# Score units of VectorE carried in ScalarE's score sets, two rings of three PSUM banks, one bank for the rest, and another order of the first loads

## The chip, the cores and the metric

The kernel runs on one core of one Trainium2 chip. The metric is the device time of that core in microseconds. Before the change three runs gave 744.49, 744.65 and 745.26 us, a median of 744.65.

## What is computed

Two attentions over the same x (2048 tokens, 512 columns, 32 heads of 16 columns), mixed by a gate. All tensors are bfloat16.

```python
def _A_ref(x, wqkv, wo):              # full attention, no mask
    qkv = (x @ wqkv).reshape(B, S, 3, H, Dh).transpose(2, 0, 3, 1, 4)
    q, k, v = qkv[0], qkv[1], qkv[2]
    p = softmax(einsum("bhqd,bhkd->bhqk", q, k) * Dh ** -0.5)
    o = einsum("bhqk,bhkd->bhqd", p, v)
    return o.transpose(0, 2, 1, 3).reshape(B, S, D) @ wo

def _B_ref(x, wqkv, wo):              # each token sees 8 tokens, 2 apart
    idx = pos[:, None] - (arange(8) * 2)[None, :]
    kg, vg = k[:, :, idx], v[:, :, idx]
    logits = einsum("bhsd,bhswd->bhsw", q, kg) * scale   # -1e9 where idx < 0
    o = einsum("bhsw,bhswd->bhsd", softmax(logits), vg)
    return o.transpose(0, 2, 1, 3).reshape(B, S, D) @ wo

g = sigmoid((x * gate_w).sum(-1, keepdims=True))
out = g * _A_ref(x, A_wqkv, A_wo) + (1 - g) * _B_ref(x, B_wqkv, B_wo)
```

## The kernel before, in words

**A planner writes the program.** The Python code holds a list of operations (`Op`) with an engine, a duration, what each depends on, a due time and the buffers (`Hold`, `Slots`) that it takes and gives back. `Sched.run` goes forward in planned time, takes for each engine the operation that can start soonest (among near ones the one due first) and emits it. `chain_on` ties each engine's instructions in that order, so the chip runs a fixed order on every engine; the chip's own semaphores decide when. `Policy` holds knobs of the planner; for each stretch of 8 us of planned time it is made from a seed in `CHOICES`. `Sched.warm` adds products with zeros where the plan has TensorE too idle.

**Full attention.** Heads come in 8 groups of four (`NG`), queries in 4 blocks of 512 (`QW`). A period is one pair of (query block, group); there are 32, in the order of `periods`. In a period the keys come in 16 tiles of 128 (`NT`). A score unit is one head, one key tile, one query block: a 32-row matmul whose 128x512 result fills one PSUM bank; TensorE runs the units of different heads in different strips of rows at once. A period has 64 units, the kernel 2048.

- ScalarE's units: `pe_source` proposes a fill of a ring (`fillA`, `emit_fill`), ScalarE reads it with one exponential over all its banks and writes `pT` (`act_source`), and TensorE multiplies `pT` with V into the period's accumulator `acc` (`emit_pva`). The rings `rA` (three banks) and `rB` (two) alternate (`ring_i`), so a set has three and two units in turn.
- VectorE's units: `start_quad` and `make_quad` take the four heads of a key tile from the back of a period, at most the last `TD` = 4 tiles. Each unit is a `fillD` on TensorE into one of two PSUM banks `m`, and a `conv` on VectorE, which makes a first term of the exponential by a multiply and an add on integers; two more terms (`term`) are adds over the whole quad (`dt`). TensorE multiplies the three terms with V and two weighted copies of V (`vd_row`, made for the last `TD` tiles by `weigh`). So a quad is four conversions and two terms on VectorE and twelve products on TensorE.

**PSUM** has eight banks: `rA` three, `rB` two, `acc` one, `m0` and `m1` one each. Everything else that TensorE makes goes through an `m` bank, and VectorE empties it: projections of K, Q and V, those of the local attention (`b_tile`), its sums (`bf2`, `vsum`) and the output projection (`final`).

**Local attention** (`b_tile`, 16 tiles of 128 tokens): K and V rows are stored to `kv_scr` in device memory and loaded again eight times shifted (`ksh`, `vsh`). GpSimd multiplies and sums; from tile `RELIEF` = 6 on, half of the sums over a head are taken by VectorE (`lred`). GpSimd and VectorE are ordered by hand (`lock`) where VectorE runs a fast operation.

**Start.** ScalarE's queue loads the weights of the first heads, ScalarE copies them into place (`wd`). `x_load` brings x transposed with eight DMA transposes on SP's queue, two halves of four. K of the first group is projected for all tokens (`k_proj` with `first`), two blocks in `m`, two in `rB`; the largest magnitude of each row (`kred`, `k_rows`) must be known for all tokens before the keys are completed (`fix`) and the first scores can be made. Q of the first block goes through `acc`.

**End.** The last query block's output projection is split: two tiles take a ring each once the last scores are read (`lent_final`, `lent_close`), two go through `m`.

Of the kernel before, what the change touches and what calls it, by code (L numbers as in the profile page):

```python
# [11 lines left out]
ALU = mybir.AluOpType  # L12
# [19 lines left out]
TD = 4  # L32
# [48 lines left out]
RELIEF = 6  # L81
# [47 lines left out]
class Policy:  # L129
    __slots__ = ("full", "press", "quads", "backlog", "heed", "near", "shift", "conv", "ring", "rng", "wobble", "warm", "tight", "late", "whole", "split")  # L130

    def __init__(self, seed):
        self.full, self.press, self.quads, self.backlog, self.heed = 5, -2000.0, 3, 3000.0, True
        self.near, self.shift, self.conv, self.ring, self.wobble, self.warm = 60.0, 0.0, -5000.0, 480.0, 0.0, 0.0
        self.tight, self.late, self.whole, self.split = 600.0, 2000.0, False, False
        self.rng = random.Random(seed)
        if seed:
# [16 lines left out]
            self.warm = pick(0.0, 0.04, 0.08, -0.03)  # L154

# [290 lines left out]
def kernel(  # L446
# [143 lines left out]
    S_.t["DVE"] = 2500.0  # L590
    S_.t["ACT"] = 2500.0
# [4 lines left out]
    def x_load(half):  # L596
# [36 lines left out]
    for kind, lo in (("k", D), ("q", 0)):  # L633
        w0[kind] = const.tile([128, DC, G1], BF16, name=f"w{kind}0")
# [11 lines left out]
    load("x0", x_load(0), 8100.0)  # L646
    load("x1", x_load(1), 13600.0)
    ld["x1a"] = S_.add(Op("SP", lambda: None, dur=1.0, due=-8.0, lat=13000.0, name="ld_x1a"))
    load("bw", dma(bw[:], B_wqkv.rearrange("(c p) n -> p c n", p=128)), 20500.0)
# [4 lines left out]
    load("gw", gw_load, 22000.0)  # L654
    load("wv", dma(wv[:, :, G1:D], a_w3[:, :, 2 * D + G1:3 * D]), 24000.0)
# [22 lines left out]
    S_.t["PE"] = 7800.0  # L678
    xt_ops = {sc: [ld[f"x{sc // 2}"]] for sc in range(NC)}
# [6 lines left out]
    def k_proj(m, sc, due, first=False):  # L686
        lent = first and sc >= 2
        if lent and not early:
            early["hold"] = Hold("rB")
        hold = early["hold"] if lent else Hold("m")  # L690
        st = {}

        def part(c0, c1):
            def s():
                if c0 == 0 and lent:
                    if sc == 2:
                        early["ps"] = ps.tile([128, 2, QW], FP32, tag="rB", bufs=1, name="ring")
                    st["pk"] = early["ps"][:, sc - 2, :]
                elif c0 == 0:
                    st["pk"] = misc_ps(hold, [128, QW])[:]  # L700
# [17 lines left out]
        slow = 2 if first and sc == 0 else 1  # L718
        p1 = Op("PE", part(0, 2), mms=COL4 * (2 * slow), deps=([ld["x1a"]] if lent else xt_ops[sc]) + [ld[("k", m)]], due=due, acq=[] if lent and sc > 2 else [hold], not_before=0.0 if first else due - 5000.0,
                begun=[early["op"]] if lent and sc > 2 else [], name="k1")  # L720
        p2 = Op("PE", part(2, DC), mms=COL4 * (2 * slow), deps=[p1] + (xt_ops[sc] if lent else []), due=due, name="k2")
        for o in (p1, p2):
            S_.add(o)
        if first:
            r = S_.add(Op("DVE", red, dur=700.0, deps=[p2], due=due, name="kred"))
            e = S_.add(Op("ACT", evac, dur=650.0, deps=[p2, r] + k_evs.get(m, [])[-1:], due=due, rel=[] if lent and sc == 2 else [hold], name="kev"))
            if lent and sc == 2:
                early["op"] = p1
            if lent and sc > 2:
                early["next"] = p2  # L730
# [78 lines left out]
    def q_proj(c_, f, due):  # L809
# [21 lines left out]
        def spread():  # L831
            v = st["qt"][:].bitcast(I32)
            V.stream_shuffle(out=v[:, 0, :], in_=v[:, 1, :], mask=LOWER)
            V.stream_shuffle(out=v[:, 1, :], in_=v[:, 1, :], mask=UPPER)

        def fold():
            for b in range(2):
                v = st["qt"][:, b, :].bitcast(U16)
                V.tensor_scalar(out=v, in0=v, scalar1=rowmask[:, b:b + 1], scalar2=None, op0=ALU.bitwise_and)
        ops = [Op("PE", part(0, 2), mms=COL4 * 2, deps=xt_ops[c_] + [ld[("q", f)]], due=due, acq=[hold, hq], name="q1"),  # L840
               Op("PE", part(2, DC), mms=COL4 * 2, due=due, name="q2"),
               Op("DVE", evac, dur=683.0, allow=300.0, rel=[hold], name="qev"),
               Op("DVE", spread, dur=860.0, allow=2000.0, name="qsh"),
               Op("DVE", fold, dur=486.0, lock=True, allow=2000.0, name="qabs")]
        S_.chain(ops)
        qb_ops[(c_, f)] = ops[1]
        for b in range(2):
            qt_ops[(c_, 2 * f + b)] = (ops[-1], hq)
# [47 lines left out]
    def b_tile(t, due):  # L896
# [190 lines left out]
        f = [Op("PE", vsum(c), mms=[("f", None, 132)] * W, allow=4000.0 if c == 0 else -3000.0, acq=[hb, obt_hold[t]] if c == 0 else [],  # L1087
# [127 lines left out]
    def lent_final(tt, due):  # L1215
# [6 lines left out]
        def step(lo, hi):  # L1222
            def s():
                if not lo:
                    lent["ps", tt] = ps.tile([128, 3 - tt, QW], FP32, tag=tag, bufs=1, name="ring")[:, 0, :]
# [126 lines left out]
    def pe_source(e):  # L1352
# [5 lines left out]
        n = 3 if ring_i[0] == 0 else 2  # L1358
        w = S_.slots[res].when()
        us = act_units(n)  # L1360
        if us and w < INF:
# [3 lines left out]
            if r < INF and S_.slots["pTA" if n == 3 else "pTB"].when() < INF:  # L1365
# [3 lines left out]
                op = Op("PE", None, mms=[("r", u[2], 512) for u in us], name="fillA")  # L1369
                op.fn = lambda us=us, res=res, n=n, op=op: emit_fill(us, res, n, op)  # L1370
# [372 lines left out]
```

## Time and profile before

| | |
|---|---|
| median of three runs | 744.65 us |
| the profiled execution: its time, its span | 744.69 us, 742.9 us |
| TensorE's granted clock | 1.00 |
| first exponential of scores starts | 19.46 us |
| exponentials of three banks, of two | 313, 312 (and one of one bank) |
| score units on ScalarE, on VectorE | 1564, 484 |
| instructions on VectorE, ScalarE, GpSimd | 1177, 658, 456 |
| GpSimd: time waited for VectorE's `dt`, ahead of `prod` | 139.9 us, in 64 waits |
| moved by DMA, mean rate | 47.42 MB, 64 GB/s |

The span is the time from the first instruction to the last of the profiled execution; its own time is 1.8 us longer. "Busy" of an engine is the time in which it runs at least one instruction; a duration reaches to an instruction's end, and on ScalarE, VectorE and TensorE the next begins before that, so durations add up to more than busy time. In a row of a group stand the line, the engine, the operation, what it writes and reads with shapes, the count, the busy time, the mean duration in ns, and the idle time of the engine just before, with what ended most of it. Every operation goes through one helper, so all rows have line 509; the tiles tell them apart. A page's group can mix shapes.

### The profile page before, as it was taken

The numbers are of one execution on the slowest core, as the hardware profiler recorded it, in microseconds if no ns is written. First come the engines' busy times: TensorE is split into PE (matmuls) and PEld (weight loads), VectorE is DVE, ScalarE is ACT, GpSimd is POOL, SyncE is SP. The second block draws the span as 40 slices with busy tenths as digits, with TensorE's granted clock in tenths as the row PEclk, the third lists the DMA queues.
The fourth block names the chain that finished last, engine by engine and source line by source line (L and its number), as shares of the span: only waits on it lengthen the run. The fifth ranks groups of instructions, "written<-read, shape, count | busy, mean of one in ns | idle before, by whom it ended". The sixth has DMA issues, their size and how long they took to land.

```text
span 742.9 us, 19546 instructions
## 1 busy us (share of the span) xinstructions
PE 695.6 (94%) x8110; PEld 247.9 (33%) x8110; DVE 652.9 (88%) x1177; ACT 719.2 (97%) x658; POOL 436.0 (59%) x456
## 2 busy tenths in 40 slices
PE   8899999999999989999999999999999999999897
PEld 2332332323323323333323333333333333323233
DVE  3888999798898898989999999989998988897963
ACT  2999999999999999999999999999999999999994
POOL 1066455756556666666655656657656557666660
PEclk9999999999999999999999999999999999999999
DMA  9413020120331201212132311121131113222100
GB/s 217 132 20 119 2 72 2 61 70 15 96 49 59 72 2 60 69 58 73 57 77 25 115 35 39 58 73 58 57 101 58 63 53 102 73 72 71 59 30 29
DMA packets 76232, 47.42 MB, mean 64 GB/s; under 512 B 37232, under 2 KB 73584, under 8 KB 76144
## 3 DMA queue, kind: packets, MB, share of 16 engines
q1 hardware_dynamic: 74288, 45.52, 20.9%
q8 instruction: 63, 1.03, 0.6%
q10 hardware_dynamic: 1856, 0.66, 0.3%
q14 instruction: 25, 0.20, 0.1%
HBM read 37.75 MB, written 6.32 MB: 59 GB/s over the span
## 4 chain that ended last, share of the span: by engine, by line
ACT 64%; PE 17%; issue 15%; DVE 5%; DVEq 0%; ACTq 0%
ACT pT L509 63%; PE m_ps L509 6%; PE acc L509 5%; PE ring L509 5%; DVE dt L509 2%; PE warm L509 1%; ACT lg L509 1%; DVE kt_all L509 0%; DVE accT L509 0%; DVE qt L509 0%; DVE kmax_all L509 0%; DVE lg L509 0%; DVE qb L509 0%; ACT kt_all L509 0%; DVE kvs L509 0%
## 5 line engine op out<-in xcount | busy, mean ns | idle before, releaser
L509 ACT ACTIVATE pT<-ring 128x1536 bf16<-128x1536 f32 x626 | 711.7, 1391 | 0.6 <-PE ring L509 0.4
L509 DVE TENSOR_SCALAR dt<-m_ps 128x512 uint16<-128x512 f32 x484 | 319.8, 680 | 32.8 <-PE m_ps L509 18.8
L509 PE MATMUL ring<-qt,kt_all 32*128 32x512 bf16 x1564 | 255.5, 381 | 36.1 <-ACT pT L509 28.8
L509 POOL TENSOR_TENSOR prod<-ksh,qb 128x512 f32<-128x512 bf16 x128 | 146.0, 1157 | 118.1 <-DVE dt L509 104.3
L509 PEld LDWEIGHTS <-kt_all 32*128 32x128 bf16 (+1 forms) x2304 | 99.9, 91 | 282.4 <-issue 265.1
L509 POOL TENSOR_TENSOR vsh<-vsh,lg 128x512 bf16<-128x512 bf16 x128 | 137.9, 1099 | 64.4 <-DVE dt L509 54.3
L509 DVE TENSOR_SCALAR dt<-dt 128x2048 uint16<-128x2048 uint16 x242 | 166.2, 702 | 3.6 <-PE acc L509 2.0
L509 PE MATMUL m_ps<-qt,kt_all 32*128 32x512 bf16 x484 | 165.3, 382 | 3.3 <-DVE dt L509 1.6
L509 PE MATMUL acc<-pT,vp_row 128*32 128x512 bf16 x1564 | 153.3, 387 | 0.7 <-DVE accT L509 0.3
L509 POOL TENSOR_TENSOR prod<-prod 128x512 f32<-128x512 f32 x88 | 96.2, 1101 | 41.1 <-DVE dt L509 35.6
L509 PEld LDWEIGHTS <-vp_row 128*32 128x32 bf16 x2048 | 49.9, 94 | 100.2 <-issue 91.2
L509 PE MATMUL acc<-dt,vd_row 128*32 128x512 bf16 x968 | 79.8, 381 | 0.0
L509 PE MATMUL m_ps<-bw,xT 128*32 128x512 bf16 x768 | 55.1, 382 | 0.1
L509 PE MATMUL acc<-dt,vp_row 128*32 128x512 bf16 x484 | 48.0, 386 | 1.1 <-DVE accT L509 1.1
L509 PEld LDWEIGHTS <-xT 128*32 128x32 bf16 (+1 forms) x1152 | 32.9, 96 | 27.3 <-issue 19.4
L509 POOL TENSOR_TENSOR ott<-accT,rden 128x256 bf16<-128x256 f32 x31 | 19.7, 635 | 33.8 <-DVE dt L509 28.0
L509 PE MATMUL m_ps<-ident,vsh 128*128 128x128 bf16 x512 | 37.4, 220 | 0.0
L509 PEld LDWEIGHTS <-vsh 128*128 128x128 bf16 x512 | 28.7, 98 | 11.8 <-issue 10.6
L509 PEld LDWEIGHTS <-vd_row 128*32 128x32 bf16 x968 | 25.0, 96 | 21.9 <-issue 9.3
L509 PE MATMUL acc<-ones_t,zw 128*32 128x512 bf16 x332 | 30.7, 387 | 0.0
L509 DVE TENSOR_REDUCE lg<-prod 128x32 f32<-128x512 f32 x40 | 26.5, 672 | 0.0
L509 DVE CAST kvs<-m_ps 128x512 bf16<-128x512 f32 x32 | 21.5, 675 | 4.6 <-PE m_ps L509 4.5
(79 smaller groups left out, 363.1 us busy)
## 6 DMA issues: line engine op xcount, KB each, us to landing
ksh<-kv_scr SPq DMA_DIRECT2D x16, 1024.0 KB, 5.7
vsh<-kv_scr SPq DMA_DIRECT2D x16, 1024.0 KB, 5.4
kv_scr<-kvs SPq DMA_DIRECT2D x16, 256.0 KB, 2.1
out_dram<-osb SPq DMA_DIRECT2D x14, 128.0 KB, 1.7
bw<-in_B_wqkv_dram SPq DMA_DIRECT2D x1, 1536.0 KB, 8.1
bwo<-in_B_wo_dram SPq DMA_DIRECT2D x1, 512.0 KB, 7.2
woarr<-in_A_wo_dram SPq DMA_DIRECT2D x8, 64.0 KB, 2.3
wv<-in_A_wqkv_dram SPq DMA_DIRECT2D x1, 384.0 KB, 8.6
```

The source lines that it names most:

```text
L509: return chain_on(key, f(*a, **k))
```

## The change

It has six parts.

1. `rB` has three banks like `rA`, and one `m` bank is left. The buffers `pT` become six of one size, shared by both rings.
2. A fill of a ring may carry one unit of VectorE (`rider`, `take_ride`): two units for ScalarE in the first two banks, one for VectorE in the third. `rider` takes it where a quad is open, its operands are there, and VectorE is planned to end the conversion within `ride` = 900 ns of the fill. `apart` declares the two readers independent. The ring is given back when both have read (`ring_read`). A unit that doesn't ride goes through `m` as before.
3. `TD` is 5, `RELIEF` is 3, the seeds in `CHOICES` are others. Quads may start from 17.5 us of planned time, before from 22.
4. The first 1024 tokens of x are loaded as they lie (`xn_load`) and transposed by TensorE with the identity (`x_turn`), through `rA`, `acc`, `rB` and `m`; ScalarE and VectorE empty them. The other 1024 come by four DMA transposes. The first projections of K use `rA`, `rB`, `m` and `acc`. GpSimd copies the first weights in place of ScalarE; three start buffers share memory with later ones. Seven warm-up matmuls accumulate in one group, before ten single ones.
5. The first Q block is emptied by ScalarE, and its two halves are spread and masked one after the other, so that the first can be used sooner.
6. The local sums (`bf2`) of the last two tiles are due 4 us earlier.

The diff, cut to its core:

```diff
-TD = 4
+TD = 5
...
-RELIEF = 6
+RELIEF = 3
...
+        self.ride = 900.0
...
-    for name_, n_ in (("m", 2), ("rA", 1), ("rB", 1), ("acc", 1), ("pTA", 3), ("pTB", 3), ("qt", 2), 
+    NPT = 6
+    for name_, n_ in (("m", 1), ("rA", 1), ("rB", 1), ("acc", 1), ("pT", NPT), ("qt", 2), 
...
+    PLAIN = 2
+    xn = work.tile([128, PLAIN * TPC, D], BF16, name="xn", tag="ksv_0", bufs=1)
+
+    def xn_load(q):
 
         def s():
-            lo, hi = half * S // 2, (half + 1) * S // 2
-            for c in range(DC):
-                SP.dma_start(out=xT[:, c, lo:hi], in_=x2d[lo:hi, c * 128:(c + 1) * 128], transpose=True)
+            SP.dma_start(out=xn[:, TPC * q:TPC * (q + 1), :], in_=x2d[q * QW:(q + 1) * QW, :].rearrange("(p t) c -> p t c", t=TPC))
+        return s
+
+    def x_load(c0, c1):
+
+        def s():
+            for c in range(c0, c1):
+                SP.dma_start(out=xT[:, c, PLAIN * QW:S], in_=x2d[PLAIN * QW:S, c * 128:(c + 1) * 128], transpose=True)
         return s
...
-            A.copy(out=o[:, c], in_=_ap(src[:, c, :], [list(src.ap[0]), [DH, 4], [4 * DH, 2], [1, DH]]))
+            G.tensor_copy(out=o[:, c], in_=_ap(src[:, c, :], [list(src.ap[0]), [DH, 4], [4 * DH, 2], [1, DH]]))
...
-    for k in range(10):
-        jt = ps.tile([128, QW], FP32, tag="acc", bufs=1, name="warm")
-        mm(jt[:], ones_t[:, 0:128], ones_t[:], True, True)
+    jt = ps.tile([128, QW], FP32, tag="acc", bufs=1, name="warm")
+    for k in range(7):
+        mm(jt[:], ones_t[:, 0:128], ones_t[:], k == 0, k == 6)
...
+    def x_turn(q, parts):
+        ends = []
+        for n_, (tag, cs, eng) in enumerate(parts):
+            hold, st = Hold(tag), {}
+
+            def turn(tag=tag, cs=cs, hold=hold, st=st):
...
+                for k, c in enumerate(cs):
+                    o = st["ps"][:, k, :].rearrange("d (p t) -> d t p", t=TPC)
+                    for tt in range(TPC):
+                        mm(o[:, tt, :], xn[:, TPC * q + tt, c * 128:(c + 1) * 128], ident[:], True, True)
+
+            def evac(cs=cs, eng=eng, st=st):
+                o, i = xT[:, cs[0]:cs[-1] + 1, q * QW:(q + 1) * QW], st["ps"][:, 0:len(cs), :]
+                if eng == "ACT":
+                    A.copy(out=o, in_=i)
+                else:
+                    V.tensor_copy(out=o, in_=i)
...
+    x_turn(0, (("rA", (0, 1, 2), "ACT"), ("acc", (3,), "DVE")))
+    x_turn(1, (("rB", (0, 1, 2), "DVE"), ("m", (3,), "ACT")))
...
-            V.tensor_copy(out=st["qt"][:, 1, :], in_=st["q"][:])
+            (A.copy if first else V.tensor_copy)(out=st["qt"][:, 1, :], in_=st["q"][:])
...
-        f = [Op("PE", vsum(c), mms=[("f", None, 132)] * W, allow=4000.0 if c == 0 else -3000.0, acq=[hb, obt_hold[t]] if c == 0 else [],
+        f = [Op("PE", vsum(c), mms=[("f", None, 132)] * W, allow=(4000.0 if t < NT - 2 else 0.0) if c == 0 else -3000.0, acq=[hb, obt_hold[t]] if c == 0 else [],
...
-        n = 3 if ring_i[0] == 0 else 2
+        n = 3
...
+                with_ = rider(us, max(r, S_.t["PE"])) if n == 3 and len(us) == 3 else None
+                if with_ is not None:
+                    us = us[:2]
...
+    def rider(us, at):
+
+        if not S_.policy.ride or S_.now < 17500.0:
+            return None
+        for q in quads_open:
+            k = next((k for k in range(4) if q["fops"][k].start is None), None)
+            if k is None:
+                continue
+            f_ = q["fops"][k]
+            if k == 0 and S_.slots["dt"].when() > at:
+                return None
+            if any(d.vis is None or d.vis > at for d in f_.deps) or any(d is not None and d.start is None for d in f_.begun):
+                return None
+            S_.guesses = {}
+            vis = at + 440.0
+            free = max(vis, S_.t["DVE"], S_.guess(q["aops"][k - 1]) if k else 0.0)
+            if free + 683.0 > vis + S_.policy.ride:
+                return None
+            used = {u[2] for u in us[:2]}
+            j = min(q["heads"], key=lambda j: (j in used, S_.pe_busy[j], j))
+            return f_, j, q, k
+        return None
+
+    def apart(peer, inst):
+
+        if peer is None:
+            return
+        if peer:
+            tc.declare_no_dep(inst.ins, peer[0].ins, reason="two engines read different banks of one set")
+        peer.append(inst)
+
+    def take_ride(op, ring, with_):
+        f_, j, q, k = with_
+        q["heads"].remove(j)
+        st = q["sts"][k]
+        st["j"], st["s"], st["peer"] = j, ring[:, 2, :], []
+        S_.pend["PE"].remove(f_)
...
+        conv = q["aops"][k]
+        conv.rel = []
+        return conv, st["peer"]
...
+    def ring_read(f_, t):
+        f_["reads"] -= 1
+        f_["free"] = max(f_["free"], t)
+        if not f_["reads"]:
+            S_.slots[f_["res"]].give(0, f_["free"])
...
-            if dve + max(0.0, S_.t["DVE"] - S_.now) < S_.policy.backlog and S_.now > 22000.0:
+            if dve + max(0.0, S_.t["DVE"] - S_.now) < S_.policy.backlog and S_.now > 17500.0:
```

More of the change, by code (lines that the diff above doesn't have):

```diff
@@ L129 @@
 class Policy:
-    __slots__ = ("full", "press", "quads", "backlog", "heed", "near", "shift", "conv", "ring", "rng", "wobble", "warm", "tight", "late", "whole", "split")
+    __slots__ = ("full", "press", "quads", "backlog", "heed", "near", "shift", "conv", "ring", "rng", "wobble", "warm", "tight", "late", "whole", "split", "ride")
     def __init__(self, seed):
@@ L686, in k_proj @@
     def k_proj(m, sc, due, first=False):
[L687 to L690, printed above, removed]
+        lent = first and sc < PLAIN
+        tag = ("rA", "rB")[sc] if lent else "acc" if first and sc == NC - 1 else "m"
+        hold = Hold(tag)
         st = {}
@@ L694, in s @@
             def s():
[L695 to L700, printed above, removed]
+                if c0 == 0:
+                    st["pk"] = ps.tile([128, 3, QW], FP32, tag=tag, bufs=1, name="ring")[:, 0, :] if lent else ps.tile([128, QW], FP32, tag="acc", bufs=1, name="p1")[:] if tag == "acc" else misc_ps(hold, [128, QW])[:]
                 pk = st["pk"]
@@ L836, in fold, with spread, s @@
-        def fold():
-            for b in range(2):
[L838 to L844, printed above, removed]
+        def spread(bs):
+            def s():
+                v = st["qt"][:].bitcast(I32)
+                for b in bs:
+                    V.stream_shuffle(out=v[:, b, :], in_=v[:, 1, :], mask=(LOWER, UPPER)[b])
+            return s
@@ L847, in q_proj @@
         for b in range(2):
-            qt_ops[(c_, 2 * f + b)] = (ops[-1], hq)
+            qt_ops[(c_, 2 * f + b)] = (ops[4 if first and not b else -1], hq)
     g_done = []
@@ L1364, in pe_source @@
                 r = max(r, qt_ops[periods[p]][0].vis, kdep(p, t).vis if kdep(p, t).vis is not None else INF)
-            if r < INF and S_.slots["pTA" if n == 3 else "pTB"].when() < INF:
+            if r < INF and sum(w_ < INF for w_ in S_.slots["pT"].free) > len(filled):
                 act_idle = S_.t["ACT"]
@@ L1700, in after_post @@
                 final(c_, tt, NPR - 1, NPR, now)
[L1703 to L1705 removed]
+    reds0 = [k_proj(0, sc, 40.0 + sc, first=True) for sc in range(NC)]
+    k_rows(0, reds0, 50.0, 1, 35000.0)
+    q_proj(0, 0, 40.5)
     for tb in (0, 8):
```

131 lines of the change are left out of this document (85 added, 46 removed), and 16 rows, old and new, of the table CHOICES.

## The prediction, made before the changed kernel was run

> **What bounds the kernel now.** I read the page first, then its groups kept apart by shape for ScalarE, the waits, the busy time in stretches, and the order of time at the start and the end.
>
> From the page:
>
> ```profile
> PE 695.6 (94%) x8110; PEld 247.9 (33%) x8110; DVE 652.9 (88%) x1177; ACT 719.2 (97%) x658; POOL 436.0 (59%) x456
> L509 ACT ACTIVATE pT<-ring 128x1536 bf16<-128x1536 f32 x626 | 711.7, 1391 | 0.6 <-PE ring L509 0.4
> L509 DVE TENSOR_SCALAR dt<-m_ps 128x512 uint16<-128x512 f32 x484 | 319.8, 680 | 32.8 <-PE m_ps L509 18.8
> L509 DVE TENSOR_SCALAR dt<-dt 128x2048 uint16<-128x2048 uint16 x242 | 166.2, 702 | 3.6 <-PE acc L509 2.0
> L509 PE MATMUL acc<-ones_t,zw 128*32 128x512 bf16 x332 | 30.7, 387 | 0.0
> ```
>
> ScalarE is the bound: its exponentials fill 711.7 of 742.9 us and it idles 0.6 us ahead of them. VectorE does 484 of the 2048 score units (121 quads of four), ScalarE the other 1564. The last row is padding that TensorE issues with nothing better to do: its 94% has 30.7 us of room.
>
> ScalarE by shape:
>
> ```profile
> L509 ACT ACTIVATE pT<-ring 128x1536 bf16<-128x1536 f32 x313 | 502.8, 1606 | 0.5 <-PE ring L509 0.4
> L509 ACT ACTIVATE pT<-ring 128x1024 bf16<-128x1024 f32 x312 | 367.3, 1177 | 0.1
> ```
>
> A third unit adds 1606 - 1177 = 429 ns. The durations overlap (502.8 + 367.3 is over 711.7), so the price of a set is what is left: 711.7 - 1564 x 0.429 = 40.7 us, over 626 instructions 65 ns, waiting included. A unit costs 0.429 us and the number of sets hardly matters.
>
> Busy time in stretches (PE, PEld, DVE, ACT, POOL), and the waits:
>
> ```profile
> 160.00:280.00 120.00, 113.37 (x1291) 39.07 (x1290) 109.45 (x200) 120.00 (x109) 73.63 (x77) 1.00 0.17 45
> 731.00:743.00 12.00, 8.03 (x141) 4.57 (x137) 4.75 (x8) 2.58 (x4) 0.00 (x0) 1.00 0.13 45
> ```
>
> ```profile
> PE ring L509 <- ACT pT L509: 28.8, 90, 0.8
> DVE dt L509 <- PE m_ps L509: 18.8, 36, 1.4
> PE m_ps L509 <- DVE dt L509: 1.6, 6, 0.4
> ```
>
> In the middle ScalarE never rests and VectorE is busy 109.45 of 120. TensorE waits for ScalarE to give a ring bank back, and almost never for VectorE: two m banks keep the two engines apart.
>
> Start and end in order of time:
>
> ```profile
> 0.72 11.14 SPq L509 DMA_TRANSPOSE xT<-in_A_x_dram  x8
> 10.77 2.46 PE L509 MATMUL m_ps<-xT,wkd 128*32 128x512 bf16 x24
> 14.60 1.91 PE L509 MATMUL ring<-xT,wkd 128*32 128x512 bf16 x32
> 18.55 1.38 DVE L509 TENSOR_SCALAR kt_all<-kt_all,rows,kadd 128x512 bf16<-128x512 bf16 x4
> 19.46 5.97 ACT L509 ACTIVATE pT<-ring 128x1536 bf16<-128x1536 f32 x5 [0.44 <-PE ring L509]
> 731.34 1.96 PE L509 MATMUL m_ps<-ident,vsh 128*128 128x128 bf16 x32
> ```
>
> So the time is three pieces in a row: 19.5 us until the first exponential, 712 of exponentials, 11 of ending. A change must move one of them.
>
> **The change part by part.**
>
> *Units moved to VectorE.* TD = 5 and the rides let VectorE take more. A quad costs it 4 x 319.8/484 + 2 x 166.2/242 = 4.02 us and saves ScalarE 4 x 0.429 = 1.72. RELIEF 3 gives VectorE 12 more reductions at 672 ns, 8.1 us, and takes tree sums from GpSimd, idle for over 300 us; the fifth weighted tile adds under 1 us. VectorE was busy 640 us from 20 to 731 us, 90% (652.9 less 7.8 and 4.8 in the ends). Of a middle of some 705 us: at 90% still, it has 635 - 640 - 9 = -14 us, 3.5 quads fewer; at 100% it has +56, 14 more. I take the middle, five more: 126 quads, 95%. What speaks for over 90% is the 32.8 us that VectorE idles ahead of score units, which now come with every set. TensorE does two more passes of four matmuls for each further quad (some 0.2 us each), 2 us for five, covered by the 30.7 us of padding; without that cover 2 us.
>
> *Sets.* The rings become three banks each and m one. With 1544 units on ScalarE and R rides there are (1544 + R)/3 sets. m can carry at most this: some 120 other evictions hold it for a 1.05 us projection and 0.69 us of reading, 210 us; what is left of 705 at 0.38 + 0.68 us a unit is 467. So R lies between 40 and 504 and the sets between 528 and 683, against 626: -6.4 to +3.7 us at 65 ns. I take R = 260, 601 sets. Exponentials: 1544 x 0.429 + 601 x 0.065 = 701.4, against 711.7: **-10.3**.
>
> *The new wait.* A ring bank set is free only when both engines have read it. Behind a fill that waits, TensorE's whole queue stands (products with V, projections), and ScalarE waits for the fill. The slack: while the other set is read (two units and the price of a set, 0.92 us) the next fill needs 0.38 and its signal, some 0.45; about 0.45 remains. A conversion late by one VectorE instruction (0.68) holds ScalarE for 0.23 us. Bounds: nothing, and every ride late, 260 x 0.23 = 60. The nearest row, units through two banks, has TensorE waiting for VectorE in 6 of 484 cases; the room is smaller now and VectorE fuller, so I take one ride in eight: 32 x 0.23, **+7.5**.
>
> The Trainium skill, "PSUM — Partial Sum Buffer", section "PSUM bank collisions raise a hardware error", says that two engines collide only on one bank and quadrant and that different banks run clean. By it the two readers cost each other nothing; no row shows two engines reading neighbouring banks of one set, and the sum is the same. Its general note to evacuate promptly speaks against the single m bank.
>
> *Start.* Half of x is loaded plainly and turned on TensorE (32 small matmuls, four evictions split over ScalarE and VectorE); four DMA transposes remain of eight. Those are issued 1.39 us apart and land 3.6 to 4.6 after issue, so the last landed near 14.2. Now two plain issues of 0.6 and three transposes stand ahead of the last: 0.7 + 1.2 + 4.2 = 6.1, landing 9.7 to 10.7. From there only 16 matmuls remain (0.95 us at the rate of the 14.60 row), two reductions at 0.69, the maximum (0.7), the first fix and the fill (0.83): about 4, first exponential near 14.2. That is -5.3. The weight copies moved from ScalarE to GpSimd (eight; nearest row there 0.43 each) end before 8 us, under the loads; the plain load's landing, 4 to 6 us, is hidden by the transposes as well.
> It hangs on TensorE's rate: the 24 matmuls at 10.77 took 2.46 us, the 32 at 14.60 only 1.91. At the slow rate the five first projections, 80 matmuls, take 8.2 us from about 8: first exponential near 18.7, -0.8. The rate rose near 12.9 us, 3.4 us after matmuls began to run unbroken at 9.5, although the ten warm-up ones, each waiting for the last, ran from 1.4. The change lets seven run unbroken and the turns follow, so I take the fast end with a little taken off: **-5.0**.
>
> The Trainium skill, "TensorE: Matmul & The Clock Gate", Part 1, has the clock rise some 3.4 to 4 us after sustained work begins. Counted from 1.4 us, the trace disagrees (still slow at 12); counted from 9.5 it agrees, and by it the change is fast from about 6 us.
>
> *End.* The last tiles' 32 matmuls (1.96 us at 731.34) stood after the last score fill, ahead of the products that close the accumulator. A due time 4 us earlier may put them under the exponentials: 0 to -2.0, I take **-1.0**; what is late next is the accumulator's transpose and the projections, as now.
>
> **Sum**: -10.3 + 7.5 - 5.0 - 1.0 = -8.8. The profiled execution took 744.7 us for its span of 742.9 (1.8 around it), the median is 744.65: forecast **735.9 us**.
>
> **The rivals.**
>
> *Late conversions hold the rings* (slower). The wait above, in ScalarE's stream: VectorE at 95% in a fixed order, with instructions ahead of a ride that wait for GpSimd or DMA. It cancels the gain at 7.5 + 8.8 = 16.3 us, 71 of 260 rides late, and decides from there. With half late: 130 x 0.23 = 30, 758 us; typically 750 to 760. For it: m's two banks hid such lateness, as the 1.6 us show. Against: a ride is taken only where VectorE is expected to end within 0.9 us of the fill, and ScalarE's own two units take 0.92.
>
> *VectorE takes no more units.* It stays near 90% with the reductions added, or the single bank starves it. 118 quads: 1576 x 0.429 + 612 x 0.065 = 715.9, +4.2; with +7.5 - 6.0 it is 750; with 121 quads 1564 x 0.429 + 608 x 0.065 = 710.5, -1.2, and 745.0. For it: 9 us in 120 idle are spread over many waits. Against: the supply of units no longer hangs on m.
>
> *VectorE nearly fills.* 132 quads: 1520 x 0.429 + 593 x 0.065 = 690.6, -21.1; with 7.5 and -6.0: 725.
>
> *Few rides happen, not what the change says.* m then carries all it can, 467 units (117 quads), with 528 sets: 1581 x 0.429 + 528 x 0.065 = 712.6, +0.9, no new wait, -6: 739.6. The order would be two-bank work through one bank, with VectorE idling ahead of dt.
>
> **How the numbers follow.** Forecast 0.48 (its own range 730 to 741); late rings 0.17 (over 746); no more units 0.16 (741 to 751); full VectorE 0.13 (721 to 730); few rides 0.06 (735 to 744). About 0.2% (1.5 us) is what a measurement can tell from no change. Faster: 0.48 + 0.13 + 0.05 + 0.07 (a part of no more units) = 0.73; same 0.06, from no more units and few rides; slower 0.17 + 0.04 = 0.21. Range 726 to 749: it leaves out most of the late rings and a part of the full case, under 2 in 10.
>
> **What would show it.** First exponential near 14.5 us; two-unit exponentials in number near R, and VectorE's conversions out of the ring by the same number; conversions in all near 504; VectorE at 94 to 95% in the middle; ScalarE's busy share near 97% but starts of exponentials apart by more than 0.9 and 1.33 us where a ring was late, in sum some 8 us above now, TensorE's ring waits named for VectorE; under 10 us from the last exponential to the end. Wrong if conversions number 484 or fewer, if the first exponential comes after 17 us, or if ring waits on VectorE exceed 16 us.

## The result and the profile after

| | before | after |
|---|---|---|
| median of the runs | 744.61 us (744.49 to 745.26) | **737.64 us** (736.08 to 738.50) |
| ratio, 95% interval | | 0.9902 [0.9884, 0.9921] |
| profiled execution: time, span | 744.69, 742.9 us | 737.22, 735.4 us |
| first exponential of scores starts | 19.46 us | 17.23 us |
| last exponential's end to the span's end | 10.7 us | 10.0 us |
| score units on ScalarE, on VectorE | 1564, 484 | 1548, 500 |
| sets of score units | 626 | 648 |

The kernel is faster by 7.0 us in the medians and by 7.5 us in the profiled executions. The forecast was 735.9 us, 8.8 below. Several of its terms were off in opposite directions, and that is what the rest is about.

The page of the changed kernel:

```profile
PE 671.7 (91%) x8163; PEld 248.6 (34%) x8163; DVE 670.3 (91%) x1220; ACT 714.7 (97%) x675; POOL 423.3 (58%) x449
L511 ACT ACTIVATE pT<-ring 128x1024 bf16<-128x1024 f32 (+1 forms) x648 | 706.4, 1338 | 2.1 <-PE ring L511 2.0
L511 DVE TENSOR_SCALAR dt<-ring 128x512 uint16<-128x512 f32 x396 | 266.5, 680 | 18.6 <-PE ring L511 15.5
L511 DVE TENSOR_SCALAR dt<-dt 128x2048 uint16<-128x2048 uint16 x250 | 170.1, 694 | 4.7 <-PE acc L511 3.9
L511 DVE TENSOR_SCALAR dt<-m_ps 128x512 uint16<-128x512 f32 x104 | 70.3, 676 | 2.0 <-PE ring L511 2.0
L511 PE MATMUL acc<-ones_t,zw 128*32 128x512 bf16 x340 | 31.1, 388 | 0.0
```

ScalarE is still the bound, 97% busy. Its exponentials fill 706.4 us, 5.3 less than before. VectorE does 396 conversions straight out of the rings and 104 through the single bank, 500 in all (484 before), and idles 20.6 us ahead of them where it had idled 32.8. TensorE is busy 24 us less than before, with the padding unchanged at 31 us.

ScalarE by shape:

```profile
L511 ACT ACTIVATE pT<-ring 128x1024 bf16<-128x1024 f32 x396 | 405.8, 1173 | 0.4 <-PE ring L511 0.3
L511 ACT ACTIVATE pT<-ring 128x1536 bf16<-128x1536 f32 x252 | 380.2, 1597 | 1.7 <-PE ring L511 1.7
```

The 396 exponentials of two banks are the sets that carry a ride, one for each conversion out of the ring. Set beside each other in their order in the trace, 393 of the 396 pairs overlap in time. The mean durations stand within 1% of those before (1177 and 1606 ns): a neighbour reading the third bank costs ScalarE nothing.

The waits that decide whether the rings are given back in time, and busy time in two stretches of the middle (length, PE, PEld, DVE, ACT, POOL, then the granted clock, the DMA share and GB/s):

```profile
PE ring L511 <- ACT pT L511: 44.8, 141, 0.8
...
PE ring L511 <- DVE dt L511: 0.9, 3, 0.5
```

```profile
160.00:280.00 120.00, 108.80 (x1296) 39.56 (x1288) 113.29 (x209) 120.00 (x112) 79.40 (x83) 1.00 0.23 63
280.00:400.00 120.00, 110.73 (x1332) 41.57 (x1333) 116.02 (x214) 120.00 (x115) 71.74 (x74) 1.00 0.18 55
```

TensorE waited for VectorE to give a ring back three times, 0.9 us in all. In these two stretches VectorE is busy 113 and 116 of 120 us (94 and 97%; 109.45 before in the first) and ScalarE never rests.

The start and the end in order of time (start, us, engine, what; in brackets the idle time before and what ended it):

```profile
0.72 0.88 SPq L511 DMA_DIRECT2D xn<-in_A_x_dram  x2
1.64 8.32 SPq L511 DMA_TRANSPOSE xT<-in_A_x_dram  x4
4.84 1.48 PE L511 MATMUL ring<-ident,xn 128*128 128x128 bf16 x12 [0.30 <-DMA xn<-in_A_x_dram]
8.52 1.05 PE L511 MATMUL ring<-xT,wkd 128*32 128x512 bf16 x16
13.75 0.40 PE L511 MATMUL m_ps<-xT,wkd 128*32 128x512 bf16 x4 [1.38 <-DMA xT<-in_A_x_dram]
16.32 1.38 DVE L511 TENSOR_SCALAR kt_all<-kt_all,rows,kadd 128x512 bf16<-128x512 bf16 x4
17.23 1.45 ACT L511 ACTIVATE pT<-ring 128x1536 bf16<-128x1536 f32 x1 [1.12 <-PE ring L511]
722.90 0.39 PE L511 MATMUL ring<-qt,kt_all 32*128 32x512 bf16 x3
723.22 1.96 PE L511 MATMUL m_ps<-ident,vsh 128*128 128x128 bf16 x32
```

The projections run at the fast rate now: 16 matmuls in 1.05 us at 8.52, where 24 took 2.46 us before. But the four transposes took 8.32 us to issue, 2.1 us each on average instead of 1.39: one of them took 3.73 us, the others 1.3 to 1.8. The last was issued only at 8.66 us, and the last piece of x reached TensorE at 13.75 us. At the end the 32 sums still stand behind the last score fill.

One thing in the profile had no counterpart before. Three stretches near the start:

```profile
18.00:20.00 2.00, 1.27 (x17) 0.83 (x17) 0.69 (x1) 2.00 (x3) 0.00 (x0) 0.50 1.06 353
22.00:24.00 2.00, 2.00 (x18) 0.39 (x19) 1.54 (x5) 1.72 (x3) 0.00 (x0) 0.50 0.03 8
24.00:26.00 2.00, 1.95 (x23) 0.37 (x19) 1.42 (x3) 1.43 (x2) 0.00 (x0) 0.79 0.00 0
```

From 18.0 to 24.8 us the granted clock is 0.50. By 22 us TensorE is the bound: it is busy 2.00 of 2.00 us, and ScalarE, which follows it, only 1.72 and 1.43.

**Waiting between exponentials.** In what follows this is a sum that I work out from the trace of ScalarE. Where nothing holds it, an exponential of three units is followed by ScalarE's next start after 1.33 us, one of two units after 0.904 us. What a start is later than that is waiting. Before it sums to 8.8 us, after to 9.5.

### The profile page after: what moved, and what is told of

Read it like the earlier page. It is cut to its first block, busy times and chain, and to the rows that moved or that the text cites. A ratio compares the mean times of both kernels' runs of the same rounds, so it can differ in the third digit from the quotient of the medians.

```text
span 735.4 us, 19595 instructions
## 1 busy us (share of the span) xinstructions
PE 671.7 (91%) x8163; PEld 248.6 (34%) x8163; DVE 670.3 (91%) x1220; ACT 714.7 (97%) x675; POOL 423.3 (58%) x449
## 3 DMA queue, kind: packets, MB, share of 16 engines
q8 instruction: 64, 1.05, 0.6%
## 4 chain that ended last, share of the span: by engine, by line
ACT 77%; issue 13%; PE 7%; SPq 1%; DVE 1%; DMA 1%; ACTq 0%; DVEq 0%
ACT pT L511 76%; PE ring L511 3%; PE acc L511 2%; PE m_ps L511 2%; ACT lg L511 1%; SPq L511 1%; DMA xT<-in_A_x_dram 1%; DVE kmax_all L511 0%; DVE dt L511 0%; DVE accT L511 0%; ACT kt_all L511 0%; DVE osb L511 0%; DVE kt_all L511 0%; DVE qt L511 0%; DVE kadd L511 0%
## 5 line engine op out<-in xcount | busy, mean ns | idle before, releaser
L511 ACT ACTIVATE pT<-ring 128x1024 bf16<-128x1024 f32 (+1 forms) x648 | 706.4, 1338 | 2.1 <-PE ring L511 2.0
L511 PE MATMUL ring<-qt,kt_all 32*128 32x512 bf16 x1944 | 265.3, 383 | 52.1 <-ACT pT L511 44.8
L511 DVE TENSOR_SCALAR dt<-ring 128x512 uint16<-128x512 f32 x396 | 266.5, 680 | 18.6 <-PE ring L511 15.5
L511 PEld LDWEIGHTS <-kt_all 32*128 32x128 bf16 (+1 forms) x2304 | 97.0, 91 | 278.8 <-issue 199.2
L511 DVE TENSOR_SCALAR dt<-dt 128x2048 uint16<-128x2048 uint16 x250 | 170.1, 694 | 4.7 <-PE acc L511 3.9
L511 PE MATMUL acc<-pT,vp_row 128*32 128x512 bf16 x1548 | 156.4, 389 | 0.7 <-ACT pT L511 0.2
L511 POOL TENSOR_TENSOR prod<-prod 128x512 f32<-128x512 f32 x76 | 83.3, 1100 | 45.7 <-DVE dt L511 42.2
L511 DVE TENSOR_SCALAR dt<-m_ps 128x512 uint16<-128x512 f32 x104 | 70.3, 676 | 2.0 <-PE ring L511 2.0
L511 PE MATMUL m_ps<-qt,kt_all 32*128 32x512 bf16 x104 | 39.6, 381 | 2.1 <-DVE dt L511 0.6
L511 DVE TENSOR_REDUCE lg<-prod 128x32 f32<-128x512 f32 x52 | 34.5, 671 | 0.0
L511 PEld LDWEIGHTS <-vsh 128*128 128x128 bf16 x512 | 28.7, 98 | 11.7 <-issue 11.0
```

Source lines behind the costliest of these rows:

```text
L511: return chain_on(key, f(*a, **k))
```

## The experiments

The ratios are to the kernel before on the same chip, whose median stood at 744.6 to 745.3 us each time.

**1. Are the two readers really apart, and what is that worth?** The declaration of independence is taken out, so that the second reader of a set waits for the first. All engines keep their order.

```diff
-            tc.declare_no_dep(inst.ins, peer[0].ins, reason="two engines read different banks of one set")
+            pass
```

> The order of every engine stays as in the changed kernel; only the declaration that the two readers of a set are independent is taken away, so that the second reader of each of the 396 shared sets waits for the first. If the independence is what makes the rides free (theory), each shared set costs ScalarE up to a conversion (0.68 us) where VectorE was emitted first, or holds VectorE by a two-unit read where ScalarE was: between 0.2 and 0.6 us a set, 396 x 0.2 to 0.6 = 80 to 240 us, so 815 to 975 us, with ScalarE's starts of two-unit sets far above 0.92 us apart. Rival (the two reads fall after one another anyway, since a ride is read late): within 5 us of 737.6.

It took 956.9 us, ratio 1.2833 [1.2798, 1.2869]. The waits:

```profile
DVE dt L511 <- ACT pT L511: 194.8, 171, 2.2
ACT pT L511 <- DVE dt L511: 142.6, 136, 1.7
```

Each engine waits for the other, and waiting between exponentials rises from 9.5 to 219.7 us, nearly the whole difference. The same plan with that wait stands 212 us above the kernel before instead of 7 below it. In the trace of the changed kernel neither of the two rows exists. Not all of it is the wait itself: with so many pauses TensorE's mean granted clock is 0.860, and ScalarE waits 44.0 us for ring fills, where it had waited 2.0. What the fallen clock adds was not separated.

**2. Do the rides carry the gain?** They are switched off in the planner; every unit of VectorE goes through the one `m` bank.

```diff
+        self.ride = 0.0
```

> No unit of VectorE rides; all go through the one m bank, the plan is made anew. Theory (rides make up for the lost m bank and for VectorE's idling): m can carry about 470 units at most beside the 120 other evictions; conversions fall below 484, to 400 to 470, all sets have three units, 527 to 550 of them; ScalarE gets 1580 to 1650 units; 745 to 775 us. Rival of the prediction (few rides matter little, the three-bank rings alone give the gain): 117 quads, 528 sets, near 739 to 740 us.

It took 889.4 us, ratio 1.193 [1.1864, 1.1996], worse than either theory allowed. Only 84 quads are done, so ScalarE has 164 units more than in the changed kernel (70 us at 0.429), and it idles 84.4 us ahead of its exponentials. The row of the `m` bank:

```profile
L512 DVE TENSOR_SCALAR dt<-m_ps 128x512 uint16<-128x512 f32 x336 | 230.2, 685 | 138.6 <-PE m_ps L512 97.5 <-PE ring L512 39.6
```

VectorE idles 138.6 us ahead of its conversions. The prediction's bound of 467 units for `m` was far too kind: with the projections and local sums between, it carried 336. This run has a flaw, though: the seeds in `CHOICES` had been chosen for a plan with rides. The next three runs answer that.

**3. The structure without chosen seeds.** The list of seeds is emptied in the kernel before and in the changed kernel, and then also in the changed kernel without rides, so that every stretch uses seed 0. The second line of the edit belongs to the third run alone.

```diff
+CHOICES = ()
...
+        self.ride = 0.0
```

> The kernel before with the planner's usual knobs in every stretch in place of the chosen seeds. Compared with the next run it tells the structure of the change from the choice of seeds. Theory (the change itself gives the time): VectorE gets 112 to 118 quads, the time lies 10 to 25 us over 745.

> The changed kernel with the usual knobs in every stretch. Theory (the structure gives the time, the seeds only polish both): 117 to 122 quads, 745 to 756 us, at least 6 us under the kernel before with the same knobs. Rival (the better time comes from better chosen seeds): within 3 us of the kernel before with the same knobs, or above it.

> The rides switched off in the changed kernel with one seed for every stretch, to be set beside the changed kernel with one seed (759.85 us, 119 quads, 358 rides), so that neither plan has had its seeds chosen. Theory, that without rides the single m bank cannot feed VectorE, whatever the seeds: fewer than 100 quads, VectorE idle ahead of m for over 60 us, TensorE padding with zeros in its place, 820 to 920 us. Rival, that most of the 152 us of the run without rides came from seeds that were chosen for another plan: more than 110 quads and 760 to 800 us, which would leave the rides a few per cent. Between them both count.

| one seed everywhere | time | ratio to the kernel before | quads | waiting between exponentials |
|---|---|---|---|---|
| kernel before | 777.66 us | 1.0430 [1.0401, 1.0460] | 114 | 31.2 us |
| changed kernel | 759.85 us | 1.0192 [1.0162, 1.0223] | 119 | 23.7 us |
| changed kernel, no rides | 901.36 us | 1.2115 [1.2070, 1.2161] | 85 | 102.9 us |

The first two runs took longer than expected (10 to 25 us over 745, and 745 to 756 us). Three things follow. With one seed on both sides the change is worth 17.8 us, more than twice what the tuned pair shows: the seeds bring the old kernel 33 us and the new one 22, so part of the gain may have been had before by choosing seeds. That is one plan on each side; how much of the 17.8 us is the luck of these two plans was not tried. The rides are what holds the structure up, with chosen seeds and with one: without them 141.5 us are lost here, of which 136 more units on ScalarE at 0.429 make 58 and the added waiting 79. And the conversions show why, in the changed kernel and in the one without rides:

```profile
L512 DVE TENSOR_SCALAR dt<-ring 128x512 uint16<-128x512 f32 x358 | 243.6, 683 | 40.5 <-PE ring L512 36.4
L512 DVE TENSOR_SCALAR dt<-m_ps 128x512 uint16<-128x512 f32 x118 | 80.1, 679 | 9.2 <-PE m_ps L512 4.8
```

```profile
L513 DVE TENSOR_SCALAR dt<-m_ps 128x512 uint16<-128x512 f32 x340 | 232.9, 685 | 139.3 <-PE m_ps L513 100.0
L513 PE MATMUL acc<-ones_t,zw 128*32 128x512 bf16 x1380 | 124.4, 402 | 0.0
```

Through the rings VectorE gets its units at 0.1 us of idling each, through one `m` bank at 0.4 us. TensorE fills the difference with zeros (124.4 us against 34.1).

**4. What would late rides cost?** The bound on a ride's lateness, 900 ns (700 or 1100 in some stretches, by their seeds), goes to 4000 ns.

```diff
+        self.ride = 4000.0
```

> The bound within which VectorE must be expected to end a ridden conversion goes from 0.9 us (0.7, 1.1 in some stretches) to 4 us, the plan is made anew. Theory (the bound is what keeps the rings free of late conversions): more rides, above 396, and many late: TensorE's ring waits on VectorE appear in tens, waiting of ScalarE between exponentials rises from 9.5 to over 20 us, 745 to 765 us. Rival (lateness has slack enough in the two rings and costs nothing): rides rise, waiting stays within 12 us, 735 to 740 us.

It took 787.88 us, ratio 1.058 [1.0561, 1.0599], more than either theory allowed.

```profile
PE ring L512 <- DVE dt L512: 26.7, 83, 1.1
...
ACT pT L512 <- PE ring L512: 47.9, 78, 2.9
```

VectorE does 131 quads, six more than in the changed kernel, and still 50 us are lost: 83 fills wait for a conversion, and ScalarE waits for those fills. So the rival of the late rings is a real mechanism, and the bound keeps it out. More quads alone are worth nothing if they come late. These seeds, too, were chosen for another plan; how much of the 50 us is theirs was not tried.

**5. The start: is it the load?** In the profile x came late, with two large weight loads next on the same queue. They are issued later.

```diff
-    load("bw", dma(bw[:], ...), 15000.0)
...
-    load("wv", dma(wv[:, :, G1:D], ...), 18000.0)
...
+    load("bw", dma(bw[:], ...), 15000.0)
+    load("wv", dma(wv[:, :, G1:D], ...), 18000.0)
+    ld["bw"].due, ld["wv"].due = 2010.0, 2020.0
```

> On SP's queue the 1.5 MB load of the local attention's weights and that of wv go behind the two small ones (gate vector, zero rows); all other orders stay. In the changed kernel the last DMA transpose was issued at 8.66 to 9.97 us, its packets were through near 11.5, and it was signalled only at 13.7, while the big load, issued at 10.0, was moving. Theory (the big load's packets hold back the last transpose's signal): signalled at 11.3 to 12.0 us, first exponential 1.7 to 2.4 us sooner, at 14.9 to 15.6 us, TensorE's idle 1.4 us at 12.4 gone, and with it perhaps the drop of its clock at 18 us; 734 to 736 us. Rival (the transpose itself is that slow): signalled near 13.7, first exponential near 17.2, 737 to 738.5 us.

It took 737.56 us, ratio 0.9898 [0.9881, 0.9914]: no change beside the 0.9902. In its profile the last transpose was there at 12.02 us and the first exponential at 15.91, near what the theory said; the time is the rival's. But nine profiles of the other experiments, with the old order of loads, have the transpose at 11.7 to 12.4 us as well. The theory falls: the late transpose of the first profile was that execution's own.

**6. The changed kernel again**, to see what belongs to one execution.

> The changed kernel itself, so that the next run has it beside it on one chip. In its first profile the last DMA transpose was signalled at 13.7 us; in five other profiles with the same order of loads (readers waiting, any ride, no ride, one seed, old end) at 11.7 to 12.1. If the late signal was an accident of that one execution: signalled near 12, first exponential at 15.4 to 16.2 us, and still 737 to 738 us, with one or two falls of the granted clock. If it belongs to the changed kernel: 13.7 and 17.2 again.

It took 737.34 us (735.86 to 738.32), ratio 0.9894 [0.9877, 0.9912]. The last transpose was there at 12.40 us and the first exponential at 15.92, 3.5 us earlier than before the change. Still the total is the same, since time was lost elsewhere:

```profile
362.90:366.30 3.40, 2.45 (x26) 0.76 (x26) 3.36 (x7) 3.40 (x4) 1.10 (x1) 1.00 0.00 0
366.30:369.70 3.40, 3.40 (x27) 0.70 (x23) 2.74 (x6) 2.94 (x4) 3.16 (x3) 0.56 0.00 0
369.70:373.10 3.40, 3.20 (x27) 0.61 (x23) 2.92 (x6) 3.01 (x4) 2.20 (x4) 0.50 0.02 5
373.10:376.50 3.40, 3.40 (x35) 0.65 (x27) 2.43 (x5) 2.35 (x3) 1.16 (x1) 0.50 0.00 0
```

After a stretch in which TensorE was busy 2.45 of 3.40 us the clock falls to 0.50 for 10.2 us, TensorE has no room left, and ScalarE drops from 3.40 to 2.35. Waiting between exponentials from 360 to 400 us is 2.9 us here and 0.4 in the first profile, where the fall was at 18 us.

**7. Keeping TensorE busy.** Ten passes of products with zeros are added where TensorE waits: four before the first projection of V, two before the first score fill, two each before the third and fourth fill. The passes are extra work. The first run has them on top of experiment 5, the second alone. The core of the edit, the same in both:

```diff
+                    for _ in range(4):
+                        mm_pass(dj[:, 0, :], True, True)
...
+        fills[0] += 1
+        if fills[0] in (3, 4):
+            dj = ps.tile([128, QW], FP32, tag="acc", bufs=1, name="warm")
+            for _ in range(2):
+                mm_pass(dj[:], True, True)
...
+        if fills[0] == 1:
+            for _ in range(2):
+                mm_pass(ring[:, 0, :], True, True)
```

> On top of the later big load: ten passes of products with zeros that TensorE does while it waits between 14 and 19 us (four before the first V projection, two before the first score fill, two each before the third and fourth); the order of all else stays. In the changed kernel and with the later big load the granted clock fell to 0.5 for 6.8 us at 18.0 and 16.2 us, and ScalarE waited some 1 us in those stretches. Theory (too little work of TensorE from 14 us on lets the clock fall, and this costs about 1 us): no fall before 40 us, waiting of ScalarE in the first 40 us down from 1.0 to under 0.4 us, 0.6 to 1.2 us less than with the later big load, 736.4 to 737.0 on the chip of that run. Rival (the fall comes whatever TensorE does there, or costs nothing): the clock falls again, time within 0.4 us of the later big load.

> The ten passes of zeros at the start alone, with the big load in its old place. With both, the time was 2.3 us under the later big load alone, and neither the fall of the clock at the start nor one at 368 us showed. Theory (the passes did it, the place of the big load does nothing): within 0.5 us of 735.3, clock 1.00 in most executions, 1.5 to 2.7 us under the changed kernel beside it. Rival (both are needed): 736.5 or more.

The first took 735.29 us, ratio 0.9871 [0.9856, 0.9886]. The second took 735.27 us, 0.9873 [0.9855, 0.9892], on the chip where the changed kernel took 737.34 beside it: 2.1 us less in the median, though the intervals of the two ratios still overlap. The same stretch in the changed kernel's first profile, in its second, and with the passes of the first run:

```profile
16.00:20.00 4.00, 2.63 (x46) 1.62 (x43) 2.24 (x7) 2.88 (x4) 0.00 (x0) 0.75 0.84 271
```

```profile
16.00:20.00 4.00, 2.59 (x56) 2.02 (x55) 1.32 (x4) 4.00 (x4) 0.00 (x0) 1.00 0.83 256
```

```profile
16.00:20.00 4.00, 3.78 (x72) 1.97 (x73) 1.54 (x4) 3.62 (x3) 0.00 (x0) 1.00 1.04 357
```

With the passes TensorE goes from 2.63 to 3.78 of 4.00 us and the clock stays at 1.00. But in the second profile it stays at 1.00 without any pass, with TensorE busy 2.59 us. Of the four profiles with these products and without passes (experiments 5 and 9 among them) three have a fall between 16 and 18 us, of the three with passes none; that the passes prevent it is likely, and not shown by so few. **No version is faster than the changed kernel with the passes alone, 735.27 us against 744.88 of the kernel before beside it.** It is no cure: one of its five executions had a mean clock of 0.991 and 738.15 us, with falls at 39.9 and 367.5 us.

**8. The fall at 367 us.** One pass of zeros more into the open accumulator before each fill that is planned between 358 and 367 us.

```diff
+        pa = last_acc[0]
+        if 358000.0 < S_.now < 367000.0 and pa is not None and npv[pa] > 0:
+            mm_pass(acc_tiles[periods[pa]], False, False)
```

> The passes at the start, and besides one pass of zeros into the open accumulator ahead of each score fill planned between 358 and 367 us, where TensorE waited for a ring and for m in the 3.4 us before the fall of the clock at 366.7. Theory (the fall in the middle comes from TensorE's waiting there, and costs ScalarE 2.9 - 0.4 = 2.5 us when it lasts 10 us): no fall near 367 in the profile, clock 1.00 in all or all but one execution, none above 736.5, median 734.3 to 735.5. Rival (it falls with the phase of something else, whatever stands there): some executions again at 0.99 with 737 to 738 us.

It took 735.44 us, ratio 0.9879 [0.9865, 0.9894], the same as without. TensorE is busier there (19.01 of 20.00 us from 360 to 380, against 17.44 in the first run of experiment 7) and this profile has no fall, but neither had that run's, nor the changed kernel's first at 17.45, and one of five executions still ran at a mean clock of 0.993, with 737.84 us. Inconclusive.

**9. The due time of the local sums.** It is set back for the last two tiles.

```diff
-allow=(4000.0 if t < NT - 2 else 0.0) if c == 0 else -3000.0
+allow=4000.0 if c == 0 else -3000.0
```

> The due time of the last two tiles' sums goes back to 4 us later; only the last matmuls change places. In the changed kernel the 32 matmuls of the last tile's sums (1.96 us) still stand right after the last score fill, because GpSimd ended the products that they read only at 721.0. Theory (the due time does nothing, GpSimd sets it): from the last exponential to the end 9.7 to 10.5 us, as with the change (10.0). Rival (the due time gave 0.7 us): 10.6 us or more.

One execution: 737.70 us. Its end:

```profile
723.24 0.39 PE L511 MATMUL ring<-qt,kt_all 32*128 32x512 bf16 x3
723.89 1.96 PE L511 MATMUL m_ps<-ident,vsh 128*128 128x128 bf16 x32
```

From the last exponential to the end it is 10.2 us, against 10.0 with the new due time. The sums stand after the last fill either way: the edit moved them by 0.3 us relative to it.

## Why the prediction was right, and where its steps were not

| term | forecast | profiled |
|---|---|---|
| start of the exponentials | -5.0 | -2.2 (19.46 to 17.23); -3.5 in the changed kernel's second profile |
| exponentials, at 0.429 a unit and 0.065 a set | -10.3 | -5.3 (711.7 to 706.4) |
| late rings | +7.5 | +0.8 (idle between exponentials 0.2 to 1.0; waiting 8.8 to 9.5, some 1.0 of it under the fallen clock) |
| end | -1.0 | -0.7 |
| sum | -8.8 | -7.5 (742.9 to 735.4) |

The middle rows are the two parts of one stretch, from the first exponential's start to the last one's end: 712.7 before, 708.2 after, -4.6. The -5.3 of busy time and the +0.8 of idle time make that up. Most of the waiting lies inside the busy time, since the durations overlap.

**Units moved to VectorE: right.** 126 quads were forecast and 125 came; VectorE at 95% of the middle was forecast, and from 20 to 722 us 93% came. The missing quad is 1.7 us.

**Sets: mechanism right, R mis-sized.** The price held: 1548 x 0.429 + 648 x 0.065 = 706.2, and the page says 706.4. But R was taken as 260, near the middle of 40 and 504, and was 396. Each ride that takes a third bank from ScalarE makes ScalarE's sets smaller, so 648 sets came instead of 601: 47 x 0.065 = 3.1 us. That and the quad are 4.8 of the 5.0 us by which the term fell short. The gain itself is 16 units fewer on ScalarE, -6.9 us, against 22 sets more than before, +1.4. The bound behind the middle value, what `m` can carry, was the weak step: without rides it carried 336 to 340 units, not 467, so some 160 units at least had to ride, not 40. That 396 did is the planner's choice, which takes a ride wherever the conditions of `rider` hold.

**The new wait: mechanism right, size far off.** It needs one ride in eight late; three fills of 648 waited, 0.9 us. What decides is the planner's bound: with 4 us in its place 83 fills wait and 50 us are lost, some of them perhaps by the seeds (experiment 4). The prediction named that bound as the argument against the late rings, and should have priced the term by it. The misses, 5.0 us too much gain here, 2.8 at the start and 0.3 at the end against 6.7 too much loss, nearly cancel; the total is right partly by luck.

The Trainium skill, "PSUM — Partial Sum Buffer", section "PSUM bank collisions raise a hardware error", says that accesses of two engines to different banks run clean. The trace agrees: 393 of the 396 shared sets were read by two engines at once, with the exponential at 1173 ns where it had been 1177.

**Start: the clock right, the loads and TensorE's remaining work wrong.** TensorE was fast from 4.3 us on (from 4.1 to 7.2 us in the twelve profiles with this start), as the prediction had it. Two steps failed. The last load was to be issued at 6.1 us and there at 9.7 to 10.7; it was issued at 8.66, since one transpose ahead of it took 3.73 us to issue, and x was complete at 11.7 to 12.4 us in most profiles and at 13.7 in the first. And "From there only 16 matmuls remain": TensorE had turns until 8.5 us and then 80 matmuls of projections, of which 48 still lay ahead at 10.2 us, so that it would not have been ready then either. The last part held: from the last landing to the first exponential it is 3.5 us in both profiles of the changed kernel, where about 4 were forecast. The first exponential comes at 15.4 to 16.5 us in the other profiles of kernels with this start, not at 14.2. The prediction called itself wrong if it came after 17 us; that holds of the first profile (17.23), not of the second (15.92).

**End: right in size, wrong in cause.** The due time does nothing beyond some 0.2 us (experiment 9, one execution); the sums did not go under the exponentials. Where the rest of the 0.7 us comes from stays open.

**The rivals.** *Late rings* and *few rides* are refuted by 0.9 us of ring waits and by 396 rides; *no more units* by 500 conversions; *nearly full VectorE* by 125 quads, though in single stretches VectorE reaches 97%. Experiment 1 shows what the change would have been had its two readers waited for each other: 957 us.

**What was not forecast** is the clock that falls. Every one of the 14 executions of the changed kernel and of its variants with the same products (experiments 5 and 9) has a mean granted clock of at most 0.995 and 735.9 to 738.5 us. Of 14 executions with the passes, 11 have at least 0.999 and 734.4 to 735.9 us; the other three have 0.991 to 0.993 and 737.0 to 738.2. So some 2 us of the gain are given back there. The kernel before is not free of it: its executions beside the experiments have mean clocks of 0.994 to 1.000. That short waits of TensorE bring the falls is supported, since executions with the passes keep the clock more often, but not shown: without passes the changed kernel's second profile has no fall at the start either, and busy time alone does not tell. There TensorE was busy 2.16 of 3.41 us from 11.70 us on and the clock held; at 362.9 us it was busy 2.45 of 3.40 us and the clock fell. Why passes at the start also go with fewer falls near 367 us stays open.

## What to carry to other kernels

A bank set may be shared by two reading engines at no cost if the program says that the readers are independent and if the slower one is bounded: here the wait hardly shows with a bound of some 0.9 us, and the plan made with 4 us took 50 us longer. Before pricing a move between two routes, find out what the route that is left can carry under its other traffic; here `m` carried 336 units instead of the 467 computed from its own times. And a comparison of two tuned kernels can understate a structure: with one seed on both sides the change was worth 17.8 us, with chosen seeds 7.

## What the runs showed of the hardware that was not expected

The granted TensorE clock falls to 0.50 in a kernel whose TensorE is 91% busy. In the profiles of the changed kernel and of its variants with passes or another order of loads the falls last 3.4, 6.8 or 10.2 us; with the waiting readers of experiment 1 some last up to 20.5 us. One of them comes after the stretch busy 2.45 of 3.40 us. They cost some 0.6 us (the one of 3.4 us) to 2.5 us (the one of 10.2 us), because TensorE at half rate holds ScalarE up. The Trainium skill, "TensorE: Matmul & The Clock Gate", Part 1, describes an activity window of some 3.4 us that runs freely, with the half rate after an idle one. The multiples of 3.4 us agree; that the half rate also follows a window with 72% busy time is this trace's.

The rate at the start goes with the form of the warm-up: ten matmuls that each waited for the last left the clock low until 12.8 us before, and with seven in one accumulation 1.0 came at 4.3 us after, at 4.1 to 7.2 us in all profiles with this start. No run changed the warm-up alone, and the turns of x follow it from 4.3 to 4.9 us on.

One of the four DMA transposes behind two plain loads took 3.73 us to issue in the first profile, and 3.3 to 3.8 us in all twelve with this start, where each of the eight before took 1.3 to 1.8. When the last one landed varied: 12.4 and 13.7 us in two executions of the same kernel, 11.7 to 13.7 us over all profiles with this start.
